# The attention weights' scaling on ScalarE instead of VectorE, in a fused window attention and softplus feed-forward kernel

## The chip, the cores and the metric

The kernel runs on one core of a Trainium2 chip. The metric is the device time of one execution in microseconds (us), as the median of several runs. A core has five engines that matter here: TensorE (PE, matrix products and transposes), VectorE (DVE), ScalarE (ACT), GpSimd (POOL) and SyncE (SP, which issues all DMAs of this kernel). Each engine executes its own queue strictly in order; between engines the queues wait for each other through semaphores.

## The reference

Attention over 8 batches, 8 heads, 576 positions and head size 64, in which each position sees itself and the 63 before it; then a feed-forward layer on the 4608 tokens.

```python
scores = scale * np.matmul(q, k.transpose(0, 1, 3, 2))
mask = (rel >= 0) & (rel < window)            # window = 64
scores = np.where(mask, scores, -1000000000.0)
scores = scores - np.max(scores, axis=-1, keepdims=True)
attn = np.exp(scores)
attn = attn / (np.sum(attn, axis=-1, keepdims=True) + 1e-09)
out = np.matmul(attn, v)                      # then x: (4608, 512)
h = x @ w_in                                  # 512 -> 2048
g = np.maximum(h, 0.0) + np.log1p(np.exp(-np.abs(h)))
return g @ w_out                              # 2048 -> 512
```

## The kernel before

The 4608 tokens are cut into 12 blocks `g` of 384, each of three tiles `j` of 128. For every block the attention is computed in four blocks of work, one for each pair of heads `hp` (48 in all); the two heads of a pair are `hh` = 0 and 1. Then come 16 steps `f` of the feed-forward layer, each over 128 of the 2048 hidden units: `ffn_up` (line 450, twelve matmuls into a PSUM bank `ps_h`), the softplus (lines 454, 455, 456 on ScalarE and 458 on VectorE, which is the last reader of `ps_h`), the split of the result into a high and a low part (460, 461), and `ffn_down` (line 471, nine matmuls into `ps_o`). Products are made of high and low parts to keep 32-bit accuracy, which is why there are three matmuls for each.

Attention of one head pair goes in stages. q and k are turned so that the head size lies on partitions: in the first two blocks by PE (`by_pe`, lines 277 and 287, evacuated by ScalarE in 282 and 293), later by splitting into bfloat16 parts (309 to 313) and a transposing DMA. Scores of a tile (line 331, or 334 in later blocks) land in a bank `ps_a` or `ps_o`. VectorE adds the mask and takes the minimum `mn` (line 342; the scores are negated). ScalarE takes the exponential of `p_t`, the weights of one head, 128 queries x 192 or 128 keys, in place, and its sum `sm` (line 345). VectorE adds 1e-9 and takes the reciprocal `rs` (352, 353). Then line 358 multiplies the weights by the reciprocal, a number for each partition, in place. PE transposes the weights (lines 379 and 380); they are evacuated (383, or 385 and 386 with a split) and multiplied with v (416, or 427). The attention's output is split into `x` (421 and 422, or 431, 432, 139 and 140), which the feed-forward layer reads. In the first two blocks lines 352 to 358 run once for the three tiles, so six scalings stand together; later they run for each tile, two scalings at a time. There are 288 scalings in all. The weights `p_t` have two sets of buffers, for even and odd head pairs.

The weights of the feed-forward layer arrive as 64-bit floats and are taken apart into two 32-bit parts by `float64_split` (161 and 166 on ScalarE, 162 to 165 on VectorE, a few of 162 and all of 167 on GpSimd). This is done for one step `f` at a time in the first part of the run.

The order of the work is made in two ways. The last lines build a list of events with due times (two units for each feed-forward step; `BASE`, `PACE`, `STG` and the like place the attention stages among the steps) and emit them in this order. On PE, what is due from 100 on is executed in exactly this order. What is due before, and everything on the other engines, is put in order by a scheduler, which goes by its own estimates of durations.

Of the kernel before, what the change touches and what calls it, by code (L numbers as in the profile page):

```python
# [12 lines left out]
AF = mybir.ActivationFunctionType  # L13
ALU = mybir.AluOpType
# [22 lines left out]
def window_attention_softplus_ffn(  # L37
# [16 lines left out]
    nc = tc.nc  # L54
# [178 lines left out]
    def attention(g, hp):  # L233
# [6 lines left out]
        def bank():  # L240
            if not odd0:
                return ps_a.tile([P, 512], F32, name="ps_a")

            taken_ps[0] += 1
            return ps_o.tile([P, 512], F32, name=f"ps_o{taken_ps[0] % NJ}")
# [76 lines left out]
        rs = att.tile([P, NJ, 2], F32, name="rs", bufs=2)  # L322
        for j in range(NJ):
            first = j == 0 and not prev
            c0 = WIN if first else 0
            n = W - c0
            sp = bank()
            spv = sp[:, : 2 * n].rearrange("p (h c) -> p h c", h=2)
            kc = slice(j * P + WIN + c0, (j + 2) * P)
            if by_pe:  # L330
                mm(spv, qt[:, j * P : (j + 1) * P], kbd[:, :, j * P + c0 : j * P + W], start=True, stop=True)
            for hh in range(0 if by_pe else 2):
                for i, (a, b) in enumerate(((0, 0), (0, 1), (1, 0))):
                    mm(  # L334
                        spv[:, hh, :], tr_q[a][:, hh, j * P : (j + 1) * P], tr_k[b][:, hh, kc],
                        start=(hh == 0 and i == 0), stop=(hh == 1 and i == 2), skip_group_check=True,
                    )
            t = ORDER[g] * NJ + j
            m = mask_b if (t * P) % S + P > S else mask
            for hh in range(2):  # L340
                pv = p_t[hh][:, j, WIN + c0 :]
                nc.vector.tensor_tensor_reduce(  # L342
                    pv, spv[:, hh, :], m[:, c0:], 1.0, 3.0e38, ALU.add, ALU.min, mn[:, j, hh : hh + 1]
                )
                nc.scalar.activation(  # L345
                    pv, pv, AF.Exp, bias=mn[:, j, hh : hh + 1], scale=-1.0, accum_out=sm[:, j, hh : hh + 1]
                )
            if by_pe and j < NJ - 1:
                yield
                continue  # L350
            jr = slice(0, NJ) if by_pe else slice(j, j + 1)
            nc.vector.tensor_scalar(rs[:, jr, :], sm[:, jr, :], 1.0e-9, None, ALU.add)  # L352
            nc.vector.reciprocal(rs[:, jr, :], rs[:, jr, :])
            for jj in range(jr.start, jr.stop):
                for hh in range(2):
                    c0 = WIN if jj == 0 and not prev else 0
                    pv = p_t[hh][:, jj, WIN + c0 :]
                    nc.vector.tensor_scalar(pv, pv, rs[:, jj, hh : hh + 1], None, ALU.mult)  # L358
            yield


# [142 lines left out]
    for g in range(NB):  # L504
        for hp in range(NP):
            if g < 3:
                base = BASE[g] + PACE[g] * hp
            else:
                base = 2 * NF * (g - 1) + SHP * hp + SH
            stages = attention(g, hp)  # L510
            for at in STG if g >= 3 else STG2 if g >= 2 else STG0:
                events.append((base + at, lambda stages=stages: next(stages, None)))
# [44 lines left out]
```

## Time and profile before

| | us |
|---|---|
| median of 3 runs | 1071.59 (1070.12 to 1072.89) |
| the profiled execution | 1069.74 |
| its span in the profile | 1067.9 |
| PE busy in the span | 1028.4 |
| DVE busy | 789.0 |
| ACT busy | 650.0 |
| POOL busy | 224.7 |
| line 358 on DVE, 288 instructions | 110.4 |
| line 345 (exponentials) on ACT, 288 instructions | 127.0 |

Times in rows are microseconds, unless "mean ns" stands in the heading of the view. A row of a group gives line, engine, operation, output and inputs with shapes, and the count; behind the bar the busy time with the mean duration in ns, and behind the next bar how long the engine was idle just before these instructions and what ended most of that. A row of stretches gives the start and end, the length, then the busy time and the count on each engine, the granted clock of PE, the share of the DMA engines and GB/s. A row of waits reads: engine, output and line, then what it waited for, then the total, the number of times and the longest. A row in order of time gives the start, the duration, the engine and the instruction, and in brackets the idle time before. PEld is the weight load of PE, which overlaps its matmuls.

### The profile page before, as it was taken

To read this page: it belongs to the slowest core of one execution; us is meant where nothing else is said; L and a number is where in the kernel's file an instruction comes from. 1 tells how busy PE (TensorE), PEld (TensorE's weight loads), DVE (VectorE), ACT (ScalarE), POOL (GpSimd) and SP (SyncE) were. 2 spreads that over 40 slices of the span, in tenths; PEclk is the share of its full clock that TensorE was granted. 3 is DMA by queue.
4 is the path that set the end of the run, shared out by engine and by line. 5 is a ranking of instruction groups with operands and counts; after the bars stand their busy time and mean duration, and the time that the engine had idled before them with its cause. 6 is when DMAs were issued, how large, how long until landed. Compare 5 with 4: busy or idle time off the path is not lost.

```text
span 1067.9 us, 18172 instructions
## 1 busy us (share of the span) xinstructions
PE 1028.4 (96%) x6096; PEld 924.3 (87%) x6096; DVE 789.0 (74%) x2319; ACT 650.0 (61%) x1669; POOL 224.7 (21%) x217
## 2 busy tenths in 40 slices
PE   7797988999999999999999999999999999999998
PEld 5576867888999899999999999999999999999996
DVE  4999899866777777777777777777777777865433
ACT  6786666666665666566656666656666665655333
POOL 4354355631111111112111111111211111110000
PEclk9999998999999999999999999999999999999999
DMA  7754645255334434343344334424434533520000
GB/s 197 198 140 105 169 105 146 67 127 119 70 71 101 96 79 105 64 97 81 81 96 96 84 76 93 107 60 88 102 74 84 115 80 62 131 51 1 30 1 30
DMA packets 296222, 98.20 MB, mean 92 GB/s; under 512 B 280512, under 2 KB 288704, under 8 KB 296128
## 3 DMA queue, kind: packets, MB, share of 16 engines
q1 hardware_dynamic: 296128, 97.03, 40.0%
q8 instruction: 48, 0.79, 0.3%
q14 instruction: 46, 0.38, 0.1%
HBM read 50.07 MB, written 10.22 MB: 56 GB/s over the span
## 4 chain that ended last, share of the span: by engine, by line
PE 78%; DVE 12%; DMA 4%; ACT 3%; issue 2%; SPq 1%; POOL 0%; DVEq 0%; ACTq 0%
PE ps_h L450 32%; PE ps_o L471 31%; PE ps_a L334 5%; PE ps_a L427 4%; PE ps_a L380 2%; DMA tr<-nat 2%; PE ps_a L379 2%; DVE p_t L358 2%; DVE osb L165 2%; DVE osb L164 1%; DVE osb L162 1%; DVE p_t L342 1%; DVE osb L163 1%; SPq L198 1%; DVE u L458 1%
## 5 line engine op out<-in xcount | busy, mean ns | idle before, releaser
L450 PE MATMUL ps_h<-x,w 128*128 128x384 f32 x2304 | 458.4, 344 | 15.4 <-DVE u L458 11.8
L471 PE MATMUL ps_o<-w,g 128*128 128x512 f32 x1728 | 438.7, 397 | 6.3 <-ACT g L460 4.3
L450 PEld LDWEIGHTS ps_h<-x,w 128*128 128x128 f32 x2304 | 400.6, 189 | 27.5 <-DVE u L458 12.5
L471 PEld LDWEIGHTS ps_o<-w,g 128*128 128x128 f32 x1728 | 318.1, 188 | 65.6 <-ACT g L460 4.6
L458 DVE SCALAR_TENSOR_TENSOR u<-ps_h,u 128x384 f32<-128x384 f32 x192 | 106.0, 552 | 139.7 <-ACT u L456 139.5
L454 ACT ACTIVATE u<-ps_h 128x384 f32<-128x384 f32 x192 | 93.6, 488 | 179.4 <-PE ps_h L450 177.2
L345 ACT ACTIVATE p_t<-p_t,mn 128x192 f32<-128x192 f32 (+1 forms) x288 | 127.0, 443 | 63.5 <-DVE mn L342 63.2
L140 POOL TENSOR_TENSOR x<-xf,x 128x384 fp32r<-128x384 f32 x40 | 41.1, 1027 | 460.6 <-DVE rs L352 362.9
L358 DVE TENSOR_SCALAR p_t<-p_t,rs 128x192 f32<-128x192 f32 (+1 forms) x288 | 110.4, 429 | 2.9
L342 DVE CUSTOM_DVE_ANT_0 p_t<-ps_a,mask 128x192 f32<-128x192 f32 (+1 forms) x244 | 77.3, 343 | 46.5 <-PE ps_a L334 36.1
L455 ACT ACTIVATE u<-u 128x384 f32<-128x384 f32 x192 | 100.7, 526 | 4.1
L456 ACT ACTIVATE u<-u 128x384 f32<-128x384 f32 x192 | 100.6, 524 | 3.2
L461 DVE TENSOR_TENSOR g<-u,g 128x384 fp32r<-128x384 f32 x160 | 89.5, 559 | 3.8 <-DVE g L460 0.5
L385 ACT CAST pt<-ps_a 128x512 fp32r<-128x512 f32 (+1 forms) x144 | 59.0, 417 | 33.7 <-PE ps_a L380 21.9
L312 POOL TENSOR_TENSOR nat<-q_in,nat 128x384 bf16<-128x384 f32 x40 | 38.6, 965 | 187.8 <-ACT nat L311 152.1
L386 DVE TENSOR_TENSOR pt<-ps_a,pt 128x512 fp32r<-128x512 f32 (+1 forms) x144 | 67.9, 477 | 12.3 <-ACT pt L385 10.7
L334 PE MATMUL ps_a<-tr 128*128 128x192 bf16 (+1 forms) x720 | 74.8, 246 | 0.9 <-DVE xf L432 0.7
L460 DVE CAST g<-u 128x384 fp32r<-128x384 f32 x176 | 67.9, 386 | 5.9
L380 PE MATMUL ps_a<-ident,p_t 128*128 128x128 f32 x276 | 66.6, 276 | 1.4 <-DVE p_t L358 1.3
L427 PEld LDWEIGHTS ps_a<-pt,vt 128*128 128x128 f32 (+1 forms) x608 | 64.0, 163 | 3.9 <-issue 0.5
L427 PE MATMUL ps_a<-pt,vt 128*128 128x64 f32 (+4 forms) x608 | 64.5, 247 | 0.4 <-DVE mn L342 0.4
L431 ACT COPY xf<-ps_a 64x384 f32<-64x384 f32 x80 | 38.1, 477 | 40.3 <-PE ps_a L427 37.5
(91 smaller groups left out, 1019.3 us busy)
## 6 DMA issues: line engine op xcount, KB each, us to landing
out_dram<-raw SPq DMA_DIRECT2D x12, 512.0 KB, 3.2
q_in<-in_q_dram SPq DMA_DIRECT2D x56, 96.0 KB, 2.6
raw<-in_moe_w_in_dram SPq DMA_DIRECT2D x10, 512.0 KB, 4.2
raw<-in_moe_w_out_dram SPq DMA_DIRECT2D x10, 512.0 KB, 4.2
k_in<-in_k_dram SPq DMA_DIRECT2D x32, 128.0 KB, 3.5
v_in<-in_v_dram SPq DMA_DIRECT2D x32, 128.0 KB, 2.8
raws<-in_moe_w_in_dram SPq DMA_DIRECT2D x6, 512.0 KB, 4.2
raws<-in_moe_w_out_dram SPq DMA_DIRECT2D x6, 512.0 KB, 5.0
```

Source lines behind the costliest of these rows:

```text
L334: mm(spv[:, hh, :], tr_q[a][:, hh, j * P : (j + 1) * P], tr_k[b][:, hh, kc], start=(hh == 0 and i == 0), stop=(hh == 1 and i == 2), skip_g ...
L342: nc.vector.tensor_tensor_reduce(pv, spv[:, hh, :], m[:, c0:], 1.0, 3.0e38, ALU.add, ALU.min, mn[:, j, hh : hh + 1])
L345: nc.scalar.activation(pv, pv, AF.Exp, bias=mn[:, j, hh : hh + 1], scale=-1.0, accum_out=sm[:, j, hh : hh + 1])
L358: nc.vector.tensor_scalar(pv, pv, rs[:, jj, hh : hh + 1], None, ALU.mult)
L427: mm(av[: D if lo else P, osl], vt[:, vb, hh, : 1 if lo else 2, :], pt[hh][lo][:, psl], start=(i == 0), stop=(i == len(order) - 1), skip_g ...
L450: mm(hv, weight(0, a, f)[:, c * P : (c + 1) * P], x[b][c], start=(i_mm == 0), stop=(i_mm == 3 * NC - 1))
L454: nc.scalar.activation(u, hv, AF.Abs)
L455: nc.scalar.activation(u, u, AF.Exp, scale=-1.0)
L456: nc.scalar.activation(u, u, AF.Ln, bias=1.0)
L458: nc.vector.scalar_tensor_tensor(gf, hv, 0.0, u, ALU.max, ALU.add)
L461: (nc.vector if g >= 2 else nc.gpsimd).tensor_tensor(gt[1], gf, gt[0].bitcast(F32), ALU.subtract)
L471: mm(ops[g][j], gt[a][:, js], weight(1, b, f), start=(first and i == 0), stop=(last and i == 2),)
```

## The change

Line 358 is issued on ScalarE as a copy with a scale, the scale being the same number for each partition. Nothing else in the source differs; the amount of work, the tiles and the DMAs are the same.

```diff
                 for hh in range(2):
                     c0 = WIN if jj == 0 and not prev else 0
                     pv = p_t[hh][:, jj, WIN + c0 :]
-                    nc.vector.tensor_scalar(pv, pv, rs[:, jj, hh : hh + 1], None, ALU.mult)
+                    nc.scalar.activation(pv, pv, AF.Copy, scale=rs[:, jj, hh : hh + 1])
             yield
```

All 288 scalings leave VectorE's queue and stand in ScalarE's. Because the scheduler places instructions, others move too: PE's order differs in the part that isn't fixed by the list of events, and the queues of the other engines are put together differently, VectorE's and ScalarE's mostly in their first quarter. The rows below of the two queues are those at the places of which the prediction speaks. On ScalarE at the start of the program, once the first head pair's exponentials are done, the order was:

```order
L345 ACTIVATE p_t_103,sm<-p_t_103,mn 128x128
L345 ACTIVATE p_t_104,sm<-p_t_104,mn 128x128
L345 ACTIVATE p_t_103,sm<-p_t_103,mn 128x192
L345 ACTIVATE p_t_104,sm<-p_t_104,mn 128x192
L383 COPY qpt<-ps_a 128x512
```

and it is now (`p_t_101` and `p_t_102` are the two heads of the first pair, `p_t_103` and `p_t_104` those of the second):

```order
L345 ACTIVATE p_t_103,sm<-p_t_103,mn 128x128
L345 ACTIVATE p_t_104,sm<-p_t_104,mn 128x128
L358 ACTIVATE p_t_101<-p_t_101,rs 128x128
L358 ACTIVATE p_t_102<-p_t_102,rs 128x128
L358 ACTIVATE p_t_101<-p_t_101,rs 128x192
L358 ACTIVATE p_t_102<-p_t_102,rs 128x192
```

Six scalings of the first pair (the last two rows come twice) stand between the second and the third exponential of the second pair. On ScalarE in the middle of the run, near 508 us of the profile before, the order was:

```order
L345 ACTIVATE p_t_103,sm<-p_t_103,mn 128x192
L345 ACTIVATE p_t_104,sm<-p_t_104,mn 128x192
L454 ACTIVATE u<-ps_h 128x384
L455 ACTIVATE u<-u 128x384
L456 ACTIVATE u<-u 128x384
```

and it is now:

```order
L345 ACTIVATE p_t_103,sm<-p_t_103,mn 128x192
L345 ACTIVATE p_t_104,sm<-p_t_104,mn 128x192
L358 ACTIVATE p_t_103<-p_t_103,rs 128x128
L358 ACTIVATE p_t_104<-p_t_104,rs 128x128
L358 ACTIVATE p_t_103<-p_t_103,rs 128x192
L358 ACTIVATE p_t_104<-p_t_104,rs 128x192
L454 ACTIVATE u<-ps_h 128x384
```

Four scalings of two tiles stand ahead of the softplus's first operation of the next step.

## The prediction

> **What bounds the kernel now.** I read the page first, then the busy times by stretch, then who keeps TensorE (PE) waiting.
>
> ```profile
> PE 1028.4 (96%) x6096; PEld 924.3 (87%) x6096; DVE 789.0 (74%) x2319; ACT 650.0 (61%) x1669; POOL 224.7 (21%) x217
> ...
> PE   7797988999999999999999999999999999999998
> DVE  4999899866777777777777777777777777865433
> ACT  6786666666665666566656666656666665655333
> ```
>
> The page's mean (PE 96%) hides two different programs. For the first eight slices of 26.7 us, VectorE (DVE) stands at 8 or 9 tenths while PE drops to 7 or 8; from the ninth on PE is full and DVE falls to 7. The stretches say it in microseconds; the columns are the length, then PE, weight loads, DVE, ScalarE (ACT) and GpSimd (POOL):
>
> ```profile
> 0.00:53.00 53.00, 39.91 (x194) 29.09 (x195) 39.54 (x136) 35.89 (x104) 22.18 (x31) 0.97 0.75 199
> 53.00:107.00 54.00, 46.22 (x240) 38.53 (x240) 53.13 (x121) 41.02 (x105) 26.15 (x21) 0.97 0.48 121
> 107.00:160.00 53.00, 46.93 (x261) 39.50 (x260) 47.91 (x111) 32.62 (x79) 25.14 (x20) 1.00 0.53 138
> 160.00:214.00 54.00, 47.20 (x265) 41.69 (x264) 49.26 (x118) 35.58 (x88) 30.00 (x23) 0.94 0.44 106
> 214.00:1000.00 786.00, 785.33 (x4834) 719.81 (x4833) 575.60 (x1791) 481.24 (x1250) 121.29 (x123) 1.00 0.40 85
> ```
>
> From 214 to 1000 us PE is idle for 786 - 785.33 = 0.7 us. Nothing taken off another engine can shorten that stretch; it can only be made worse. From 53 to 214 us (161 us) DVE is busy for 53.13 + 47.91 + 49.26 = 150.3 us, ACT for 109.2, PE for 140.4, so PE lacks 20.6 us. What it lacks them for:
>
> ```profile
> L450 PE MATMUL ps_h<-x,w 128*128 128x384 f32 x2304 | 458.4, 344 | 15.4 <-DVE u L458 11.8
> ...
> PE ps_h L450 <- DVE u L458: 1.7, 2, 0.9
> ...
> PE ps_h L450 <- DVE u L458: 4.7, 3, 2.8
> ...
> PE ps_h L450 <- DVE u L458: 5.4, 3, 2.5
> ```
>
> The last three rows are the waits of 53-107, 107-160 and 160-214 us; they add up to the 11.8 us of the whole run. The up-projection waits for a PSUM bank that line 458 on DVE must read, and line 458 stands in DVE's queue behind other work. So the start-up is bound by DVE, and the rest by PE.
>
> **What the change takes from DVE.** The scalings, by the same stretches (time on DVE, count):
>
> ```profile
> 0.00:53.00 53.00, 11.75 (x30) 0.97 0.75 199
> 53.00:107.00 54.00, 7.92 (x18) 0.97 0.48 121
> 107.00:160.00 53.00, 6.17 (x12) 1.00 0.53 138
> 160.00:214.00 54.00, 7.20 (x11) 0.94 0.44 106
> 214.00:1000.00 786.00, 77.41 (x218) 1.00 0.40 85
> ```
>
> In the bound stretch 53-214 us these are 41 instructions and 7.92 + 6.17 + 7.20 = 21.3 us, 14% of DVE's 150.3. Not all of that need come back, because part of it is not work:
>
> ```profile
> 14.71 1.40 DVE L358 TENSOR_SCALAR p_t<-p_t,rs 128x128 f32<-128x128 f32 x6
> ...
> 25.22 1.27 DVE L163 TENSOR_SCALAR osb<-osb 128x512 uint32<-128x512 uint32 x1
> ...
> 28.61 3.10 DVE L358 TENSOR_SCALAR p_t<-p_t,rs 128x128 f32<-128x128 f32 x6
> ...
> 36.65 0.41 DVE L163 TENSOR_SCALAR osb<-osb 128x512 uint32<-128x512 uint32 x1
> ...
> 28.75 1.61 POOL L162 TENSOR_SCALAR osb<-osb 128x512 f32<-128x512 f32 x1 [2.53 <-ACT osb L161]
> 30.33 1.26 POOL L167 TENSOR_TENSOR w<-osb,w 128x512 fp32r<-128x512 f32 x1
> ```
>
> Six scalings take 1.40 us alone (0.23 each) and 3.10 us where POOL runs two instructions over them; line 163 shows the same, 0.41 against 1.27 us. If a delay that POOL causes merely lands on DVE's next instruction of this sort, the change frees only 41 x 0.23 = 9.6 us of the 21.3. The Trainium skill ("SBUF — State Buffer", Who interferes with whom) says that DVE in a two-port mode and GpSimd hold a shared port pair exclusively, and the second to issue blocks; by that rule the lower figure is the safer one, and ACT, with ports of its own, would not be stretched. Both ends are kept below.
>
> **What it puts on ACT.** No row shows this operation on ACT. The nearest are the exponential on the same tiles, which also takes a per-partition operand, and the plain copies of line 385:
>
> ```profile
> L345 ACT ACTIVATE p_t<-p_t,mn 128x192 f32<-128x192 f32 x256 | 114.5, 450 | 55.2 <-DVE mn L342 54.9
> ...
> L385 ACT CAST pt<-ps_a 128x512 fp32r<-128x512 f32 x80 | 46.9, 586 | 22.4 <-PE ps_a L380 21.9
> ...
> L385 ACT CAST pt<-ps_a 128x64 fp32r<-128x64 f32 x64 | 13.2, 206 | 11.3 <-PE ps_a L379 11.2
> ...
> 508.43 0.44 ACT L345 ACTIVATE p_t<-p_t,mn 128x192 f32<-128x192 f32 x1
> 508.77 0.19 ACT L345 ACTIVATION_READ_ACCUMULATOR p_t<-p_t,mn 128x1 f32 x1
> 508.87 0.44 ACT L345 ACTIVATE p_t<-p_t,mn 128x192 f32<-128x192 f32 x1
> ```
>
> The exponential lasts 450 ns but overlaps what follows: from its start to its accumulator read pass 508.77 - 508.43 = 0.34 us, to the next exponential 0.44. The scaling has no accumulator read, so 0.35 us of queue time is my value and 0.44 the upper bound. Below, line 385 on a straight line from 206 ns (64 wide) to 586 (512) gives 315 ns at 192, less the same 0.10 us overlap 0.21. The exponential is the nearer row, for it has the pointer operand and these tiles. All 288 add 288 x 0.35 = 101 us to ACT.
>
> **The first stretch, 0 to 53 us.** ACT gets 30 x 0.35 = 10.5 us on top of 35.89, so 46.4 of 53. It could not start sooner:
>
> ```profile
> 0.00:11.67 11.67, 7.00 (x18) 4.03 (x18) 1.80 (x12) 5.12 (x13) 8.20 (x21) 1.00 0.66 150
> ...
> 17.91 0.17 DVE L352 TENSOR_SCALAR rs<-sm 128x6 f32<-128x6 f32 x1 [0.57 <-ACT p_t L345]
> 18.11 0.19 DVE L353 RECIPROCAL rs<-rs 128x6 f32<-128x6 f32 x1
> 18.34 1.40 DVE L358 TENSOR_SCALAR p_t<-p_t,rs 128x128 f32<-128x128 f32 x6
> ```
>
> By 11.67 us ACT has done 5.12 us; the other 30.77 and the 10.5 added end at 11.67 + 41.3 = 52.9 at the earliest. A scaling still waits for the sum and the reciprocal on DVE, 18.34 - 17.91 = 0.43 us a group; five groups, if nothing fills ACT meanwhile, make 2.2 us and 55.1. So this stretch becomes bound by ACT and I put it at +2 us (2.1 over its 53). At worst ACT keeps all the 41.33 - 30.77 = 10.6 us that it idled after 11.67, and the stretch grows by the whole 10.5.
>
> What is queued behind the waiting scalings is in the order on ScalarE at the program's start, shown with the change above. The next pair's four remaining exponentials, and the evacuation of the transposes (line 383) that makes this pair's attention output, now stand behind six scalings on the one engine; before, two engines shared them.
>
> **53 to 214 us.** DVE goes from 150.3 to between 129.0 and 140.7 us of 161, ACT from 109.2 to 109.2 + 41 x 0.35 = 123.6, PE stays at 140.4. DVE is no longer the fullest, and ACT doesn't take its place: PE does. I expect line 458 to come out of its shorter queue in time and count the 11.8 us of PE's waits for it as won, 12 with the small ones; at most all 20.6 us of PE's idle time.
>
> **214 us on.** 218 x 0.35 = 76 us go onto ACT's 481.2 of 786 (71%), and PE must still never wait. The place where I see it tightest is a step with two score tiles, the second order shown above (near 508 us). Four scalings have moved ahead of the first reader of the next up-projection. In the trace that reader waits there for PE:
>
> ```profile
> 511.05 0.49 ACT L454 ACTIVATE u<-ps_h 128x384 f32<-128x384 f32 x1 [1.65 <-PE ps_h L450]
> ...
> ACT u L454 <- PE ps_h L450: 139.2, 81, 2.9
> ```
>
> 4 x 0.35 = 1.4 us fit into 1.65; the second row says that from 214 to 1000 us ACT has 139.2 us of such waits against the 76 added. I cost this stretch at nothing; at the upper 0.44 the four need 1.76 us and line 454 would be 0.1 us late. Without that cover the 76 us would be on PE's path.
>
> **The sum.** +2 (0-53) - 12 (53-214) + 0 = -10 us. The profiled execution took 1069.74 us, 1.9 below the median 1071.59 and inside the three runs (1070.12 to 1072.89): it would become 1059.7, the median 1061.6. I forecast **1062 us**, with 1055 to 1068 for this case by itself.
>
> **The rivals.**
> - *The start-up's contention stays.* Only 9.6 of 21.3 us come free on DVE, so 45% of the 12: -5.4 + 2 = -3.4, 1068 us. For it: the 1.27 us of line 163. Against it: half of all scalings last 315 ns or less, close to the shortest, so aren't contended at all (row below).
> - *ACT becomes the start-up's bound, and the kernel is slower.* Place: the queue shown at the start. ACT keeps its idle time, +10.5 in 0-53. In 53-107 it keeps the 13 us that it idles now, and its 18 x 0.35 = 6.3 come on top; 107-214 wins 0.65 of its 10.1 us of waits, 6.6. Together +10.2, 1082 us. It decides when ACT is over about nine tenths busy in 53-107 (by the sum it would be 47.3 of 54, 88%, just below). For it: one queue now carries exponential and scaling in series. Against it: of ACT's 68.9 us of idle time before 214 us (214 less 35.89 + 41.02 + 32.62 + 35.58), 30.8 are two waits for DVE (rows below), whose queue gets shorter. The Trainium skill ("ScalarE: Activation LUTs", Rules for kernel authors) says to use VectorE, not ScalarE, for a multiply; that is this rival's side. The rows agree that one scaling is dearer on ACT: 0.23 us uncontended on DVE against my 0.35.
> - *The late stretch loses.* If line 454 comes 0.25 us late twice in each of the 218 / 6 = 36 head-pair blocks and PE feels it, 18 us are added: 1080 us. Against it: 1.4 in 1.65.
> - *A larger win.* PE loses all its 20.6 us of idle time: 1071.6 - 20.6 + 2 = 1053 us, or less.
>
> The rows for the two arguments against, of the whole run (least, median and longest duration in ns) and of ACT's waits in 0-214 us:
>
> ```profile
> L358 DVE TENSOR_SCALAR p_t<-p_t,rs x288: 274/315/1423, 14.7 to 973.7; 128x192 f32<-128x192 f32 x128, 128x128 f32<-128x128 f32 x16
> ...
> ACT p_t L345 <- DVE mn L342: 16.6, 13, 2.8
> ACT w L166 <- DVE osb L165: 14.2, 14, 2.9
> ```
>
> **How the numbers follow.** Forecast 0.53, contention stays 0.16, ACT bound 0.15, late loss 0.07, larger win 0.09. A change under about 0.3% (3.2 us) can't be told from none. Faster takes the forecast, the larger win and a third of the contention case: 0.53 + 0.09 + 0.05 = 0.67; same the rest of that case, 0.11; slower the two losses, 0.22. The range 1050 to 1079 leaves out the far ends of the losses and of the win, some 0.2.
>
> **What would show it.** Right: DVE under 88% busy in 53-214 us, ACT near 77%, the waits of line 450 for line 458 under 4 us instead of 11.8, PE full from about 205 us instead of 214, the scaling on ACT at 0.35 us from start to start. Wrong: the first line 454 (the first up-projection's evacuation) well after 55 us, PE waiting in the start-up for ACT lines where it waited for DVE, or PE idle by more than 3 us between 214 and 1000.

## The result and the profile after

The changed kernel takes 1082.45 us in the median (1081.37 to 1084.11), the kernel before 1071.49 (1070.12 to 1072.89) beside it. The ratio is 1.0106, with a 95% interval of 1.0093 to 1.0119: 1% slower, where 1062 us and a gain were forecast. The span of the profiled execution is 1082.3 us, before it was 1067.9. These two differ by 14.4 us where the medians differ by 11.0: the profiled execution of the changed kernel (1084.11 us) was the longest of its four, 1.7 us above the median, the one before (1069.74) 1.9 below the median on record with it. So differences read from these two traces can be too large by up to 3.4 us.

The totals and the slices on the page of the changed kernel:

```profile
PE 1032.4 (95%) x6096; PEld 928.3 (86%) x6096; DVE 694.7 (64%) x2031; ACT 746.0 (69%) x1957; POOL 220.8 (20%) x217
...
PE   6788878899999999999999999999999999999998
...
DVE  4897699555667666566666656666666666665433
ACT  7998667567667677776767767776677777765433
```

The work moved as intended: 94 us left DVE and 96 came to ACT. From the ninth slice on PE is full as it was. Most of the loss lies in the first eight. The stretches of the changed kernel, with the same columns as in the prediction:

```profile
0.00:53.00 53.00, 38.11 (x174) 27.70 (x174) 34.29 (x107) 43.63 (x128) 23.68 (x32) 0.94 0.77 205
53.00:107.00 54.00, 46.17 (x235) 38.80 (x236) 47.46 (x105) 47.79 (x129) 26.76 (x21) 0.97 0.48 127
107.00:160.00 53.00, 41.53 (x232) 35.10 (x231) 43.00 (x95) 34.04 (x86) 19.85 (x17) 0.94 0.50 134
160.00:214.00 54.00, 47.15 (x259) 41.38 (x258) 42.52 (x94) 35.75 (x87) 26.87 (x23) 0.97 0.39 96
214.00:1000.00 786.00, 782.29 (x4814) 716.40 (x4814) 497.36 (x1573) 555.50 (x1476) 122.65 (x124) 1.00 0.40 85
```

In 107 to 160 us no engine is full: PE 41.5 of 53, DVE 43.0, ACT 34.0. That isn't a bound that went from one engine to another. Three engines wait for each other in turn. The starts of line 454, one for each feed-forward step, tell where the time went (a table made from the two traces, in us):

| nth line 454 | before | changed | later by |
|---|---|---|---|
| 1 | 53.4 | 55.6 | 2.2 |
| 7 | 97.5 | 98.6 | 1.1 |
| 10 | 115.7 | 119.2 | 3.5 |
| 12 | 125.1 | 140.1 | 15.0 |
| 33 | 249.6 | 259.2 | 9.6 |
| 192, the last | 1058.2 | 1072.6 | 14.4 |

Between the 10th and the 12th, 11.5 us are lost; part of that comes back by the 33rd, and another 4.8 us are lost after it. ScalarE's queue in the changed kernel where this begins, in order of time (start, duration, instruction):

```profile
118.43 0.47 ACT L454 ACTIVATE u<-ps_h 128x384 f32<-128x384 f32 x1
118.80 0.44 ACT L345 ACTIVATE p_t<-p_t,mn 128x192 f32<-128x192 f32 x1
...
119.24 0.47 ACT L454 ACTIVATE u<-ps_h 128x384 f32<-128x384 f32 x1
119.61 0.79 ACT L358 ACTIVATE p_t<-p_t,rs 128x192 f32<-128x192 f32 x2
120.30 0.51 ACT L455 ACTIVATE u<-u 128x384 f32<-128x384 f32 x1
...
121.59 0.65 ACT L161 ACTIVATE osb<-raw 128x512 f32<-128x512 f32 x1
122.13 0.51 ACT L455 ACTIVATE u<-u 128x384 f32<-128x384 f32 x1
122.55 0.79 ACT L358 ACTIVATE p_t<-p_t,rs 128x192 f32<-128x192 f32 x2
...
123.33 0.53 ACT L456 ACTIVATE u<-u 128x384 f32<-128x384 f32 x1
123.75 0.65 ACT L161 ACTIVATE osb<-raw 128x512 f32<-128x512 f32 x1
124.31 0.79 ACT L358 ACTIVATE p_t<-p_t,rs 128x192 f32<-128x192 f32 x2
125.00 0.51 ACT L456 ACTIVATE u<-u 128x384 f32<-128x384 f32 x1
```

The softplus (454, 455, 456) of the 9th and 10th step is laced through with scalings, exponentials and the weights' split. The 9th runs from 118.43 to 123.86 us, 5.4 us for 1.5 us of work, the 10th from 119.24 to 125.51, 6.3 us. The same two steps in the kernel before, first and last line of each:

```profile
113.86 0.48 ACT L454 ACTIVATE u<-ps_h 128x384 f32<-128x384 f32 x1
...
115.27 0.53 ACT L456 ACTIVATE u<-u 128x384 f32<-128x384 f32 x1
115.69 0.48 ACT L454 ACTIVATE u<-ps_h 128x384 f32<-128x384 f32 x1
...
118.42 0.51 ACT L456 ACTIVATE u<-u 128x384 f32<-128x384 f32 x1
```

There they took 1.9 and 3.2 us. Groups of the changed kernel, over the whole run:

```profile
L450 PE MATMUL ps_h<-x,w 128*128 128x384 f32 x2304 | 461.5, 345 | 19.3 <-DVE u L458 14.0
...
L358 ACT ACTIVATE p_t<-p_t,rs 128x192 f32<-128x192 f32 (+1 forms) x288 | 109.1, 439 | 11.8 <-DVE rs L353 8.1
...
L379 PE MATMUL ps_a<-ident,p_t 128*128 128x128 f32 x248 | 61.1, 276 | 3.9 <-ACT p_t L358 3.9
```

The waits for line 458 didn't fall from 11.8 to under 4 us; they rose to 14.0, and PE waits for the scalings on ACT besides. Of the late 4.8 us, 3.2 can be seen as waits of PE at the changes of blocks near 511 us (1.66 us) and near 762 us (1.53 us). Here is the first, in order of time with the idle time in brackets:

```profile
509.92 0.52 ACT L309 ACTIVATE nat<-q_in 128x384 bf16<-128x384 f32 x1 [1.64 <-DMA tr<-nat]
...
510.47 0.56 DVE L310 SCALAR_TENSOR_TENSOR q_in<-q_in,nat 128x384 f32<-128x384 f32 x1 [1.20 <-ACT nat L309]
511.12 0.55 DVE L461 TENSOR_TENSOR g<-u,g 128x384 fp32r<-128x384 f32 x1
...
511.73 1.90 PE L471 MATMUL ps_o<-w,g 128*128 128x512 f32 x7 [1.66 <-DVE g L461]
```

On VectorE line 461, which PE needs, now stands behind line 310, which waits for ScalarE, which waits for a transposing DMA. In the kernel before, 461 stood ahead of 310.

### The profile page after: what moved, and what is told of

It reads as the page before. It is cut to its first block, busy times and chain, and to the rows that moved or that the text cites. A ratio compares the mean times of both kernels' runs of the same rounds, so it can differ in the third digit from the quotient of the medians.

```text
span 1082.3 us, 18281 instructions
## 1 busy us (share of the span) xinstructions
PE 1032.4 (95%) x6096; PEld 928.3 (86%) x6096; DVE 694.7 (64%) x2031; ACT 746.0 (69%) x1957; POOL 220.8 (20%) x217
## 4 chain that ended last, share of the span: by engine, by line
PE 83%; DVE 8%; ACT 3%; DMA 2%; SPq 2%; issue 2%; POOL 0%; DVEq 0%; ACTq 0%
PE ps_o L471 34%; PE ps_h L450 34%; PE ps_a L334 5%; PE ps_a L427 4%; PE ps_a L380 2%; PE ps_a L379 2%; DVE osb L164 1%; DVE osb L165 1%; DMA raw<-in_moe_w_out_dram 1%; DVE osb L162 1%; SPq L204 1%; DMA tr<-nat 1%; DVE osb L163 1%; ACT p_t L345 1%; DVE u L458 1%
## 5 line engine op out<-in xcount | busy, mean ns | idle before, releaser
L358 ACT ACTIVATE p_t<-p_t,rs 128x192 f32<-128x192 f32 (+1 forms) x288 | 109.1, 439 | 11.8 <-DVE rs L353 8.1
L380 PE MATMUL ps_a<-ident,p_t 128*128 128x128 f32 x276 | 67.0, 277 | 2.0 <-ACT p_t L358 1.2
L379 PE MATMUL ps_a<-ident,p_t 128*128 128x128 f32 x248 | 61.1, 276 | 3.9 <-ACT p_t L358 3.9
```

The source lines that it names most:

```text
L358: nc.scalar.activation(pv, pv, AF.Copy, scale=rs[:, jj, hh : hh + 1])
L380: tp(pp[:, j * W : j * W + P], p_t[hh][:, j, P:], ident)
```

## The experiments

The first theory was that not the scaling on ScalarE loses the time, but the order into which the scheduler then puts all queues. To part the two, a table was added that gives the order of a queue; each instruction is declared to follow the one ahead of it, which ties the scheduler's hands and adds no semaphore. Below, "before's order" is the order of the queues in the kernel before, "after's order" that in the changed kernel. The core of that edit, used by all kernels below with an order "held" (the table itself, rows of numbers, is left out):

```diff
+    follow(tc)
...
+def follow(tc):
...
+    for queue in zlib.decompress(base64.b85decode("".join(TABLE))).decode().split(";"):
+        at, last = 0, None
+        for step in queue.split(","):
+            at += int(step)
+            name = f"I-{at}"
+            if last is not None:
+                tc.add_manual_dep(found[name], last, info, reason="order table")
+            last = name
```

A scaling that changes its engine is put into the other queue where it began in the trace of the kernel whose order is held. All ratios below are to the kernel before, with their 95% intervals.

| kernel | median us | ratio |
|---|---|---|
| changed | 1082.45 | 1.0106 [1.0093, 1.0119] |
| before's order in all queues, scalings on ScalarE | 1069.08 | 0.9986 [0.9976, 0.9996] |
| after's order in all queues, scalings on VectorE | 1092.46 | 1.0203 [1.0187, 1.0219] |
| on ScalarE in the first two blocks only | 1083.01 | 1.0110 [1.0093, 1.0127] |
| on ScalarE from the third block only | 1073.93 | 1.0031 [1.0019, 1.0043] |
| scalings on VectorE, the two heads in reversed order | 1076.71 | 1.0046 [1.0029, 1.0063] |
| only PE's order held | 1088.65 | 1.0158 [1.0140, 1.0175] |
| the four other orders held | 1071.02 | 1.0000 [0.9990, 1.0010] |
| only ScalarE's order held | 1071.68 | 1.0016 [1.0007, 1.0026] |
| only VectorE's order held | 1077.07 | 1.0073 [1.0053, 1.0092] |
| VectorE's and ScalarE's held | 1073.96 | 1.0035 [1.0021, 1.0050] |
| ScalarE's held up to 117 us | 1078.12 | 1.0072 [1.0056, 1.0087] |
| ScalarE's held from 117 us on | 1083.42 | 1.0115 [1.0098, 1.0133] |
| after's order, late pair moved | 1081.47 | 1.0092 [1.0077, 1.0107] |
| one column on VectorE, before's order | 1060.29 | 0.9915 [0.9900, 0.9930] |
| one column on ScalarE, before's order | 1063.88 | 0.9942 [0.9927, 0.9956] |
| one head on each engine, before's order | 1065.99 | 0.9957 [0.9941, 0.9974] |

### Engine and order apart

The changed line with the order of the kernel before in all five queues:

```diff
-                    nc.vector.tensor_scalar(pv, pv, rs[:, jj, hh : hh + 1], None, ALU.mult)
+                    nc.scalar.activation(pv, pv, AF.Copy, scale=rs[:, jj, hh : hh + 1])
...
+    follow(tc)
```

> All 288 scalings on ScalarE, but every engine's queue in the order of the kernel before (a table of instruction numbers that the scheduler has to follow); each scaling stands in ScalarE's queue at the place that its start time in the trace of before gives it. Theory ORDER (the loss comes from the queues that the scheduler put together anew): at or below the kernel before, 1060 to 1073 us, and PE's waits for L358 and L461 near nothing. Theory ENGINE (one queue for exponential and scaling costs the time): most of the 11 us stay, 1078 to 1085 us.

And the line of the kernel before, with the order of the changed kernel:

```diff
                     nc.vector.tensor_scalar(pv, pv, rs[:, jj, hh : hh + 1], None, ALU.mult)
...
+    follow(tc)
```

> The other corner: all 288 scalings on VectorE as before, but every queue in the order that the changed kernel has; each scaling stands in VectorE's queue at the place that its start time in the trace of the changed kernel gives it. ORDER: slow, 1077 to 1086 us, although no scaling is on ScalarE. ENGINE: near the kernel before, 1069 to 1074 us.

In before's order the scaling on ScalarE is a small gain (1071.06 to 1069.08 us, the interval of the ratio ends at 0.9996); in after's order it is a larger one (1092.46 to 1082.45). The order costs 13.4 us with the scaling on ScalarE (1082.45 - 1069.08) and 21.4 with it on VectorE. So the move to ScalarE doesn't lose time in either order. The new order does. Two limits of this comparison: in each held kernel with a moved scaling, the scalings stand where the other engine's trace put them, which may not be their best places; and after's order on VectorE was slower than either theory had it (1086 us at most). That holding an order costs little by itself is borne out by the kernel below with the late pair moved: after's order held but for two instructions takes 1081.47 us, the free one 1082.45.

The gain of the move is still only 2 us, not 10. The stretch 53 to 214 us of the kernel with before's order and the scaling on ScalarE, then its waits there:

```profile
53.00:214.00 161.00, 144.24 (x775) 125.38 (x774) 139.11 (x309) 122.74 (x313) 79.97 (x63) 0.94 0.48 122
```

```profile
PE ps_h L450 <- DVE u L458: 10.0, 6, 3.2
...
DVE u L458 <- ACT u L456: 5.9, 6, 1.6
```

In the kernel before, the same view gives for the second of these:

```profile
DVE u L458 <- ACT u L456: 0.9, 2, 0.7
```

Line 458 does come to the head of its queue sooner, and then stands there for the softplus on ScalarE: 5.9 us where it was 0.9. PE's wait for line 458 only fell from 11.8 to 10.0 us. PE's waits for the scalings, expected near nothing, rose: lines 379 and 380 wait 4.3 us for line 358 from 0 to 214 us, before 2.1. And of the 21.3 us of scalings taken from DVE in this stretch, 150.31 - 139.11 = 11.2 came free. Part of the difference is visible on line 163, before and then with the scaling on ScalarE in before's order (whole run):

```profile
L163 DVE TENSOR_SCALAR osb<-osb 128x512 uint32<-128x512 uint32 x32 | 20.2, 631 | 0.9 <-POOL osb L162 0.7
```

```profile
L163 DVE TENSOR_SCALAR osb<-osb 128x512 uint32<-128x512 uint32 x32 | 23.6, 737 | 0.3
```

The same 32 instructions take 3.4 us more. In the traces of both kernels, every one of them with nothing on POOL at the same time takes 0.43 us or less, and every one that takes over 0.6 has an instruction of POOL over it; there are 10 of these before and 14 now. That fits the prediction's lower bound, by which a delay lands on another instruction of DVE; that these are the same delays isn't shown.

### Which part of the run

The source asks for the block: scalings of the first two blocks on ScalarE, or all others.

```diff
-                    nc.vector.tensor_scalar(pv, pv, rs[:, jj, hh : hh + 1], None, ALU.mult)
+                    if g < 2:
+                        nc.scalar.activation(pv, pv, AF.Copy, scale=rs[:, jj, hh : hh + 1])
+                    else:
+                        nc.vector.tensor_scalar(pv, pv, rs[:, jj, hh : hh + 1], None, ALU.mult)
```

> The scheduler is free again. Scalings on ScalarE only in the first two blocks (g < 2, 48 of 288), where six stand together. ENGINE: the start is where ScalarE is fullest, so most of the start-up's loss, +6 to +10 us, 1077 to 1082 us. ORDER: no size follows from the number of scalings; anything from 1060 to 1085 us, but PE's queue before 240 us must differ from the one before.

The other kernel has `g >= 2` in this place.

> The scheduler is free. Scalings on ScalarE only from the third block on (g >= 2, 240 of 288). ENGINE: the start-up keeps its time, the two late stalls of 2 us and what goes with them stay, +4 to +5 us, 1075 to 1077 us. ORDER: the late stalls stay if VectorE's queue again has L461 behind L310 at the block changes, +4 us; the start-up is open.

The first two blocks bring the whole loss (1083.01 us), the other ten 2.9 us (1073.93). Since the scheduler makes a new order for each of these kernels, they show where an edit upsets it, not what a scaling costs. The second kernel's 2.9 us are a difference of two things in its trace: the 33rd feed-forward step starts 2.3 us earlier than before (247.4 for 249.6), and the steps from there to the last take 815.7 us, 7.1 more than before.

### An edit that changes nothing but the order of two equal instructions

```diff
-                for hh in range(2):
+                for hh in (1, 0):
```

> The kernel before, all scalings on VectorE, with the two heads of a pair scaled in the other order (1, then 0): the same instructions on the same engines, and the scheduler is free. It puts the queues together about as differently as the engine change does (PE's queue alike in the tail, another order in the first quarter). ORDER in its strong form (any edit draws a new order, worth up to some 20 us): 1075 to 1090 us. If the engine change itself is what makes the scheduler's order bad (its estimates for ScalarE are off): 1068 to 1074 us.

The scalings stay on VectorE, and the kernel is 0.46% slower. In its trace the first line 454 starts at 49.5 us (before: 53.4) and the 12th at 135.1 (before: 125.1). An edit that leaves the work and its engines as they were thus moves this kernel by 5 us through the order alone. That is less than half of the 13.4 us; whether the engine change draws a worse order by chance, or because the scheduler's estimates for ScalarE are off, one such edit doesn't tell.

### Which queue carries it

To the changed kernel the same lines are added, with a smaller table. It holds PE's queue only, or the four others and not PE's:

```diff
                     nc.scalar.activation(pv, pv, AF.Copy, scale=rs[:, jj, hh : hh + 1])
...
+    follow(tc)
```

> Scalings on ScalarE; only PE's queue is held in the order of the kernel before, the other queues are the scheduler's. If PE's order makes the loss (transposes that wait for scalings placed ahead of up-projections): 1069 to 1074 us. If it is the order on ScalarE and VectorE (the softplus behind scalings and weight splits): 1078 to 1085 us.

> The complement: scalings on ScalarE; the queues of VectorE, ScalarE, GpSimd and SP are held in the order of the kernel before, PE's is the scheduler's. PE's order at fault: 1078 to 1085 us. The others' order at fault: 1069 to 1074 us.

Holding PE's queue doesn't help (1088.65 us), holding the other four removes the loss (1071.02). Then, with the same edit, the table holds ScalarE's queue, VectorE's, or both:

> Scalings on ScalarE; only ScalarE's queue is held in the order of the kernel before (with the scalings put in where they began in its trace), the other four queues are left to the scheduler. Theory: the loss sits in ScalarE's new queue, where softplus operations stand behind scalings and exponentials, so holding this one queue brings the time to 1068 to 1074 us. Rival: the loss sits in VectorE's queue, or in how the queues fit together; then holding one queue doesn't help, 1079 us or more.

> Scalings on ScalarE; only VectorE's queue is held in the order of the kernel before, the others are left to the scheduler. Theory (the loss sits in ScalarE's queue): no help, 1079 us or more. Rival (it sits in VectorE's queue, which carries line 458): 1068 to 1074 us. If both this and the run that holds ScalarE's queue stay above 1079, no single queue carries it and the fit between queues does.

> Scalings on ScalarE; the queues of VectorE and ScalarE are both held in the order of the kernel before, those of PE, GpSimd and SyncE left to the scheduler. Theory: these two queues are all that matters, 1069 to 1074 us, like the kernel with four queues held (1071.0). Rival: the order of the DMA issues or of GpSimd counts as well, 1077 us or more.

ScalarE's queue alone brings 1071.68 us, 10.8 of the 13.4; VectorE's alone half of that. Every kernel in which all of ScalarE's queue is held in before's order lies between 1069 and 1074 us, every other one with all scalings on ScalarE at 1077 or more. Holding VectorE's queue as well doesn't help further (1073.96). With ScalarE's queue alone held, the instructions of PE and VectorE come in an order that is neither before's nor after's; so the run shows that holding this queue is enough, and not that the other queues' new orders did no harm. PE's groups with ScalarE's queue held show something besides:

```profile
L450 PE MATMUL ps_h<-x,w 128*128 128x384 f32 x2304 | 456.1, 344 | 6.8 <-DVE u L458 3.3
```

Here the waits for line 458 did fall, to 3.3 us, as the forecast wanted. The kernel isn't faster than before for it: other waits stand in their place. From PE's waits of 0 to 214 us, of which the kernel before has 0.6 and 0.4 us:

```profile
PE ps_a L416 <- ACT qpt L383: 3.7, 4, 1.7
...
PE ps_a L427 <- DVE mn L342: 2.6, 1, 2.6
```

The last question on the queue was whether one part of it is enough. With the same edit, the table holds its first 213 instructions, or those from the 214th on:

> Scalings on ScalarE; of ScalarE's queue the first 213 instructions (up to about 117 us) are held in the order of the kernel before, the rest and all other queues are left to the scheduler. Theory: the loss arises after 117 us, where softplus operations of three steps stand behind scalings, exponentials and the weights' split (the 11th and 12th line 454 came 11 and 15 us late), so holding the first part doesn't help, 1078 us or more. Rival: the early order brings it about, 1068 to 1075 us.

> Scalings on ScalarE; of ScalarE's queue all from the 214th instruction on (from about 117 us) are held in the order of the kernel before, the first part and all other queues are left to the scheduler. Theory: the loss arises there, 1069 to 1075 us. Rival: it arises before, 1078 us or more.

Neither is enough (1078.12 and 1083.42 us). The theory that the loss arises after 117 us falls with the second: though the queue is held from there on, nothing comes back in the median. Holding the first part brings back 4.3 us; in its trace the 33rd line 454 starts at 254.6 us (changed: 259.2, before: 249.6), and the late waits for line 461 are still there (2.9 us). So these runs don't tie the loss to one place. A kernel with half of an order held gets a new other half, and that can be bad as well.

### The late loss

The two lines 461 that stood behind line 310 are moved back to stand right behind their line 460; all else stays in after's order. VectorE's queue at the first of them:

```diff
-L310 SCALAR_TENSOR_TENSOR q_in<-q_in,nat 128x384
-L313 COPY nat<-nat 128x6x64
 L461 TENSOR_TENSOR g<-u,g 128x384
+L310 SCALAR_TENSOR_TENSOR q_in<-q_in,nat 128x384
+L313 COPY nat<-nat 128x6x64
```

> The changed kernel in its own order, but for two instructions: at the two block changes where VectorE's queue has L461 (low part) behind L310 (which waits for ScalarE and a transposing DMA), L461 stands right behind L460 again. If these two waits of PE (1.7 and 1.5 us, with 0.3 each before) are the whole loss behind 260 us, 3.5 to 4.5 us come back: 1078 to 1079 us. If PE loses them elsewhere, 1081 to 1083.

Near 511 us the changed place reads, in order of time:

```profile
510.37 0.56 DVE L461 TENSOR_TENSOR g<-u,g 128x384 fp32r<-128x384 f32 x1
510.39 2.48 PE L471 MATMUL ps_o<-w,g 128*128 128x512 f32 x9 [0.26 <-DVE g L460]
```

PE's wait of 1.66 us for line 461 is gone. From the 33rd line 454 to the last pass 809.9 us, where the changed kernel needs 813.4 and the one before 808.6: 3.5 of the 4.8 us. The median fell by only 1.0 us. In this profile the start-up was 1.1 us slower than in the changed kernel's (33rd at 260.3 for 259.2), so the span shows 2.4. The medians differ by less still because the profiled execution of the changed kernel lay 1.7 us above its median and this one 0.3; where the rest of the 3.5 us went isn't settled. By the traces, 3.5 us of the late loss come from these two instructions; the medians don't show it.

### What relief of VectorE is worth, and what ScalarE charges

Before's order in all queues; each scaling multiplies only the first column of its tile and leaves the others out. First on VectorE:

```diff
-                    nc.vector.tensor_scalar(pv, pv, rs[:, jj, hh : hh + 1], None, ALU.mult)
+                    nc.vector.tensor_scalar(pv[:, 0:1], pv[:, 0:1], rs[:, jj, hh : hh + 1], None, ALU.mult)
```

> The order of the kernel before in all queues, scalings on VectorE, but each multiplies only the first column of its tile (the other columns are left out), so VectorE is relieved of most of its 110 us while ScalarE is not loaded. Theory: with ScalarE loaded the waits of line 450 for line 458 stayed at 10.0 us because line 458 now waited for the softplus on ScalarE (line 456, 5.9 us); with ScalarE free they fall to 2 to 6 us, and the time is 1058 to 1066 us. Rival: the start-up's pace is set by something that neither engine's scalings touch (the split of the weights across three engines, the transfers), and relieving VectorE is worth little: waits of 9 us or more, 1067 to 1071 us.

```profile
L450 PE MATMUL ps_h<-x,w 128*128 128x384 f32 x2304 | 459.8, 345 | 14.0 <-DVE u L458 10.3
...
L358 DVE TENSOR_SCALAR p_t<-p_t,rs 128x1 f32<-128x1 f32 x288 | 46.5, 207 | 2.9
```

VectorE's scalings shrink by 110.4 - 46.5 = 64 us and no other engine gets more to do: 1060.29 us, 0.85% faster. The theory had the time right and the reason wrong, since the waits for line 458 stayed at 10.3 us, though line 458 now waited less for the softplus on ScalarE (53 to 214 us; it was 5.9 with all scalings there):

```profile
DVE u L458 <- ACT u L456: 2.3, 5, 0.7
```

So that wait is not what held PE's waits up. The gain lies elsewhere, half of it ahead of the first feed-forward step. The first line 454, in the kernel before and here:

```profile
53.42 0.85 ACT L454 ACTIVATE u<-ps_h 128x384 f32<-128x384 f32 x2
```

```profile
48.52 0.84 ACT L454 ACTIVATE u<-ps_h 128x384 f32<-128x384 f32 x2
```

4.9 us are won by the first, 4.5 more by the 33rd (240.2 for 249.6), none later. The same on ScalarE:

```diff
-                    nc.scalar.activation(pv, pv, AF.Copy, scale=rs[:, jj, hh : hh + 1])
+                    nc.scalar.activation(pv[:, 0:1], pv[:, 0:1], AF.Copy, scale=rs[:, jj, hh : hh + 1])
```

> The order of the kernel before in all queues, scalings on ScalarE, but each multiplies only the first column of its tile (the other columns are left out). Theory: what ScalarE's load costs is the time of the scalings on its queue, so with much shorter ones most of the 9 us between 1060.3 (one column on VectorE) and 1069.1 (all on ScalarE) goes, 1060 to 1065 us. Rival: it costs by where the scalings stand, the engine waiting in order for sums and reciprocals of VectorE, 1067 to 1070 us.

```profile
L358 ACT ACTIVATE p_t<-p_t,rs 128x1 f32<-128x1 f32 x288 | 72.0, 285 | 17.6 <-DVE rs L353 13.5 <-DVE rs L352 1.0
```

In order of time, near 511 us:

```profile
510.82 0.29 ACT L358 ACTIVATE p_t<-p_t,rs 128x1 f32<-128x1 f32 x1
511.02 0.51 ACT L455 ACTIVATE u<-u 128x384 f32<-128x384 f32 x1
```

One column takes 0.20 us of the queue (511.02 - 510.82), a whole scaling 0.35. The starts of line 454 in the four kernels with before's order, next to the kernel before:

| scaling | first | 33rd | last |
|---|---|---|---|
| on VectorE (before) | 53.4 | 249.6 | 1058.2 |
| one column on VectorE | 48.5 | 240.2 | 1049.0 |
| one column on ScalarE | 50.7 | 243.8 | 1052.2 |
| on ScalarE | 53.9 | 248.6 | 1057.0 |
| one head on each | 51.8 | 246.2 | 1055.0 |

ScalarE's price is the distance from the second row to the fourth: 8.0 us at the last step, 5.4 of them already at the first. With one column it is 3.2. It falls with the time that the scalings take on ScalarE's queue, as the theory had it, and a rest stays even for the shortest of them. These prices are net: in the second row VectorE still has 46.5 us of one-column scalings, which in the third and fourth are gone from it, so if that relief is worth anything, the load on ScalarE costs more by as much.

### A version that beats both

```diff
-                    nc.vector.tensor_scalar(pv, pv, rs[:, jj, hh : hh + 1], None, ALU.mult)
+                    nc.vector.tensor_scalar(pv, pv, rs[:, jj, hh : hh + 1], None, ALU.mult) if hh else nc.scalar.activation(pv, pv, AF.Copy, scale=rs[:, jj, hh : hh + 1])
```

> The order of the kernel before in all queues; the scaling of the first head of a pair on ScalarE, of the second on VectorE. Theory: what VectorE's relief brings and what ScalarE's load costs both go by the number of scalings, so half of them gives half of each, 1069 to 1071 us, between the kernel before and the one with all on ScalarE (1069.1). Rival: both engines have slack for half a load, and the two heads run side by side, 1062 to 1067 us, the fastest of the kernels that compute everything.

```profile
L358 DVE TENSOR_SCALAR p_t<-p_t,rs 128x192 f32<-128x192 f32 (+1 forms) x144 | 72.5, 513 | 2.8
...
L358 ACT ACTIVATE p_t<-p_t,rs 128x192 f32<-128x192 f32 (+1 forms) x144 | 63.4, 444 | 24.5 <-DVE rs L353 20.6 <-DVE rs L352 0.8
```

With before's order held, one head on each engine gives 1065.99 us, 0.43% faster than before and the fastest of the kernels that compute everything. It is the rival that holds. By halves of each, the last line 454 would start midway between before (1058.2) and all on ScalarE (1057.0), at 1057.6 us; it starts at 1055.0. Whether half the load costs less than half or half the relief brings more isn't told apart by this run. The scalings left on VectorE take longer there (72.5 us for 144; all 288 took 110.4), and it is faster all the same.

## Why the prediction was wrong, point by point

**The step that failed is that the change was costed in the order of the kernel before.** The prediction showed two places where the scheduler had changed ScalarE's queue, costed those, and gave the order of the rest no term of its own in the sum and no rival. It is worth 13.4 us with the scaling on ScalarE, and all of the loss. At the first of these places, and at a later one of the same sort just ahead of the first up-projection's evacuation (line 454), the changed kernel's trace reads:

```profile
13.70 2.06 ACT L358 ACTIVATE p_t<-p_t,rs 128x128 f32<-128x128 f32 x6
15.67 0.44 ACT L345 ACTIVATE p_t<-p_t,mn 128x192 f32<-128x192 f32 x1
...
53.50 2.07 ACT L358 ACTIVATE p_t<-p_t,rs 128x128 f32<-128x128 f32 x6
55.60 0.88 ACT L454 ACTIVATE u<-ps_h 128x384 f32<-128x384 f32 x2
```

**The price of a scaling on ACT, 0.35 us: right.** Six begin at 53.50 and line 454 2.10 us later, 0.35 each; at 13.70 the six take 15.67 - 13.70 = 1.97 us, 0.33 each.

**0 to 53 us, +2: the size fits, its make-up doesn't.** The first line 454 came 2.2 us late. With the order held it is 0.5. The prediction counted VectorE's relief here as nothing; the one-column kernel shows 4.9 us, and ScalarE's load takes 5.4 back.

**What comes free on DVE, 9.6 to 21.3 us: near the low end.** 11.2 us, with the order held. The Trainium skill ("SBUF — State Buffer", Who interferes with whom) has GpSimd and VectorE block each other on a shared port pair; that fits line 163, which does the same work and got 3.4 us longer, though which instruction blocked which is not in the trace.

**53 to 214 us, -12: wrong also with the order held.** "I expect line 458 to come out of its shorter queue in time": it reached the head of its queue, and then waited 5.9 us for line 456; but with ScalarE unloaded that wait was 2.3 us and PE's waits for line 458 were 10.3 all the same. What keeps line 458 late isn't settled. From the first to the 33rd line 454 the move gains 1.5 us ((249.6 - 53.4) - (248.6 - 53.9)), with ScalarE unloaded 4.5. Taking a group of waits as the gain to be had was the error: with ScalarE's queue held they fell to 3.3 us and nothing was won; in the one-column kernel they stayed and 9.2 us were won.

**214 us on, 0: right for the move, wrong for the change.** With before's order PE is busy for 785.40 of 786 us there and the last 159 steps take 808.4 us (before: 808.6), so the scalings there, 76 us on ACT, cost nothing. The changed kernel needs 813.4, and 3.5 of these 4.8 us came from two instructions in VectorE's queue, an engine that the prediction didn't look at in this stretch.

**"Use VectorE, not ScalarE", the rule of the Trainium skill ("ScalarE: Activation LUTs", Rules for kernel authors): right on the operation, not on this kernel.** Whole scalings on ScalarE charged 8.0 us net by the last step, against the 9.2 that the relief of VectorE by one-column scalings brought; so in the same order the move was nearly even, and no loss.

**The rival "ACT becomes the start-up's bound", 1082 us, has the number and not the mechanism.** It put 6.3 us into 53 to 107, where the steps lost nothing (the 7th line 454 is 1.1 us late, the first was 2.2), and a gain into 107 to 214, where the loss is and ACT is busy for 34.0 of 53 us.

**The rival "the start-up's contention stays", 1068 us, has the number of the move, not of the change.** With before's order held, 11.2 us came free on DVE (it said 9.6) and the kernel takes 1069.08 us. But it got its time from 5.4 us of PE's waits for line 458, and they fell by 1.8; so its nearness is in part luck. The rival "the late stretch loses" looked at line 454 on ScalarE; the late loss, 4.8 us where it had 18, came mostly by line 461 on VectorE.

**Not all signs that the prediction named told the two cases apart.** DVE under 88% in 53 to 214: it is 83% (47.46 + 43.00 + 42.52 of 161) in the slower kernel and 86% (139.11) with before's order, so this share says nothing of the time. The waits of line 450 for line 458, 14.0 us and not under 4, spoke against the forecast, and two of the signs for wrong came: the waits for ACT lines, and PE idle by 786 - 782.29 = 3.7 us late in the run.

What isn't settled: which turns of ScalarE's order lose the time, and how much of it the other queues' orders lose with it. The laced softplus above is where the loss begins in the trace; that it is the cause was argued, and the two runs that held half of the queue didn't confirm a place.

## What to carry to other kernels

Where a scheduler orders the queues, a change of one line is two changes, the work moved and the new order, and the second can be several times the first: hold the old order, or make an edit of the same place that changes only the order of equal instructions, before a time is put down to the work. A wait that stands in front of the full engine needn't be what its removal is worth; ask what the waiting instruction will wait for next. A load split between two engines can beat either one alone.

## What the runs showed of the hardware

The same matmul isn't equally long in all start-ups. The kernel before, then before's order with the scaling on ScalarE, then after's order with the scaling on VectorE, groups of 53 to 214 us:

```profile
L450 PE MATMUL ps_h<-x,w 128*128 128x384 f32 x296 | 63.4, 355 | 12.5 <-DVE u L458 11.8 <-POOL w L167 0.6
```

```profile
L450 PE MATMUL ps_h<-x,w 128*128 128x384 f32 x299 | 66.8, 367 | 10.9 <-DVE u L458 10.0 <-ACT w L166 0.9
```

```profile
L450 PE MATMUL ps_h<-x,w 128*128 128x384 f32 x250 | 58.3, 374 | 16.6 <-DVE u L458 13.4 <-ACT x L421 2.2 <-DVE x L422 0.9
```

The mean goes from 355 over 367 to 374 ns as the granted clock of that stretch goes from 0.97 over 0.94 to 0.92. In the second kernel 299 x 12 ns = 3.6 us of PE's time went this way, nearly as much as PE's idle time fell (161 - 140.34 = 20.7 to 161 - 144.24 = 16.8 us). The Trainium skill ("TensorE: Matmul & The Clock Gate", Part 1) says that the clock is granted by how busy PE has lately been. By PE's idle time over the stretch the runs don't show that: the kernel before has the higher clock with the longer idle time. These are single executions, and the clock wasn't varied by itself.

Most of a scaling's duration doesn't go with its width: one column of 128 partitions takes 285 ns on ScalarE and 207 on VectorE, a whole tile 439 on ScalarE (row of line 358 above).
